# Block spectra of a convolution: tiles of u before tiles of r, and where decoded weights lie meanwhile

## The chip, the core and the metric

The kernel runs on one core of a Trainium2 chip. The metric is the device time of one execution in microseconds (us). A core has five engines with a queue each: TensorE (PE) for matmuls, VectorE (DVE), ScalarE (ACT), GpSimd (POOL) and SyncE (SP), which only sends transfers. Transfers of SP, ACT and POOL run on 16 DMA engines that all share.

## The reference

```python
h_mlp = np.maximum(pos_emb @ w1, 0.0) @ w2
h_filt = h_mlp * np.exp(-0.01 * pos)[:, None]
u = x * v
Uf = np.fft.rfft(u, n=2 * S, axis=1)
Hf = np.fft.rfft(h_filt, n=2 * S, axis=0)
y = np.fft.irfft(Uf * Hf[None, :, :], n=2 * S, axis=1)[:, :S, :]
...
x = (x * y)
h = x @ w_in
g = np.where(h > 0.0, h, np.exp(np.minimum(h, 0.0)) - 1.0)
x = g @ w_out
...
h = x @ w2_in
g = np.maximum(h, 0.0) + alpha * np.minimum(h, 0.0)
out = g @ w2_out
```

There are S = 12480 rows of 128 columns; the inner width of both MLPs is 2048. The weights of the MLPs come as 64-bit floats.

## The kernel before, in words

The Fourier transforms are done as matmuls in two steps. Rows are cut into 98 blocks of 64 positions for each of two halves; the block spectra come first. Three stages follow each other, and the change lies in the first.

**Stage A, positions.** `load_pos` loads the transposed position embeddings into the big region `ureg`. `r_group(g)`, eight times, multiplies them by w1 on PE (eight matmuls) and evicts the result through a Relu to `rreg`, half on ACT, half on DVE. The result is called r: 64 channels of the filter's hidden layer.

**Stage A, block spectra.** `a_tile` takes four channels, does four matmuls with a cosine and sine matrix, and evicts real and imaginary parts. There are 32 tiles of u (128 channels of x times v), written to `ureg`, and 16 tiles of r, written to the regions `sa` and `sb`; every tile of r writes into all of `sa` and `sb`, in strides. The buffers in PSUM are four (`psa`). The list `order` (line 243) alternates: two tiles of u, one of r.

**The ring of x and v.** `load_u(k)` loads x and v of tile k, 98 rows of 2 KB each, on SP's queue; there are five places for x and three for v. `mul_u(k)` multiplies them in the place of x, on POOL, and for every sixth tile on DVE. After tile k of u has been issued, x of tile k+5 is requested (it waits until PE has read tile k), the product of tile k+3 is issued, and v of tile k+6 is requested (it waits until a product has freed a place). SP sends in order, so a transfer that waits holds up all behind it.

**Decoding.** The weights are 16 pieces of 512 KB. `dec_load(j)` loads piece j on SP's queue; `dec_op(j, i)`, eleven steps, turns it into a high and a low part in float32r with six operations on DVE, two on ACT and two on POOL, and writes the two parts to DRAM as another 512 KB (`wd`, pieces 0 to 2 from POOL's queue, 3 to 8 from ACT's). Pieces 0 to 2 are decoded during the position groups, 3 to 8 during the block spectra, 9 at the start of the next stage. `hooks` holds at which tile which step is issued, and `fixed` holds where a piece lies: `ureg`, `dreg`, and columns of `rreg` that are free once their tiles of r have been done.

**Stage B** (`b_r`, `b_u`, `b_h`, `products`, `z_mm`, 25 rounds) finishes the spectra, multiplies them and starts the way back. It starts with `b_r(0)`, which reads the first frequencies of `sa` for all channels, and loads four pieces of the matrix g ahead (`load_g`). **Stage C** is the rest: the last inverse step and both MLPs, tile after tile.

Of the kernel before, what the change touches and what calls it, by code (L numbers as in the profile page):

```python
# [9 lines left out]
F32 = mybir.dt.float32  # L10
# [9 lines left out]
P = 64  # L20
NI = 98
# [4 lines left out]
NF = 99  # L26
# [13 lines left out]
def kernel(ctx: ExitStack, tc: tile.TileContext, posT, w1b, w2b, sc2, xva, xT,  # L40
# [4 lines left out]
    def pool(name, bufs=1, **kw):  # L45
        return tc.tile_pool(name=name, bufs=bufs, reuse_waits="tile", **kw)
# [16 lines left out]
    def col(o, n):  # L63
        return ureg[:, o : o + n]
# [11 lines left out]
    f_sb = fpool.tile([NI, 2 * NF], F32, name="f_sb")  # L76
    dreg = fpool.tile([128, 2048], F32, name="dreg")
    sc_sb = fpool.tile([128, 1], F32, name="sc_sb")
    ups = pb.enter_context(pool("ups", 4, side="right"))
    psa = pb.enter_context(pool("psa", 4, space=PSUM))  # L80


# [51 lines left out]
    def halves(t):  # L134
        return t[:, :1024], t[:, 1024:2048]
# [19 lines left out]
    def load_u(k, t=(0, 1)):  # L155
        for c in t:
            if k < NU:
                u_raw[k, c] = ups.tile([NI, 4, 2, P], F32, name="xv"[c], bufs=(5, 3)[c])
                nc.sync.dma_start(u_raw[k, c].rearrange("i c a p -> i (c a p)"),
                                  xva[:, c, 4 * k : 4 * k + 4].rearrange("i c a p -> i (c a p)"))  # L160

# [7 lines left out]
    def load_pos(g, n=1):  # L169
        nc.sync.dma_start(col(g * GW, n * GW), posT[:, g * GW : (g + n) * GW])  # L170
# [11 lines left out]
            else:  # L182
                nc.scalar.activation(dst, src, AF.Relu)

    w1_sb = col(NG * GW + 4096, 128)
    nc.scalar.dma_start(w1_sb, w1b)
    load_pos(0)
    nc.scalar.dma_start(sc_sb, sc2)
    load_pos(1)
    for j in range(3):  # L190
        fixed[j] = halves(col(NG * GW + 2048 * j, 2048) if j < 2 else dreg)
    dec_load(0)
    load_pos(2, 2)
    dec_load(1)
    load_pos(4, 2)
    nc.sync.dma_start(f_sb, fmat)
    load_u(0)
    load_pos(6, 2)
    load_u(1)
    load_pos(8, 2)  # L200
    dec_load(2)
    load_pos(10, 2)
    load_u(2)
    load_pos(12, 2)
    load_pos(14, 2)
    load_u(3)
    load_u(4)
    nc.sync.dma_start(fw_sb[:NI, : 2 * NF], fwin)
    nc.sync.dma_start(w2_sb, w2b)
    load_u(5, (1,))  # L210
    hooks = {3: [(mul_u, (0,))], 4: [(mul_u, (1,))], 6: [(mul_u, (2, nc.vector))]}
    for j, s in enumerate((0, 1, 4)):
        for i, d in enumerate((0, 0, 0, 0, 0, 0, 0, 1, 1, 1, 2)):
            hooks.setdefault(s + d, []).append((dec_op, (j, i)))
    for g in range(NG // 2):
# [24 lines left out]
                else:  # L240
                    nc.scalar.activation(o, x, AF.Copy, scale=scale)

    order = []
    for k in range(CC // 4):
        order += [(0, 2 * k), (0, 2 * k + 1), (1, k)]
    order = order[:-3] + [order[-1]] + order[-3:-1]

    rfree = [halves(rreg[:, 2048 * x : 2048 * x + 2048]) for x in range(2)]
    fixed.update({9: rfree[1], 3: halves(dreg), 4: rfree[0], 5: halves(dreg), 6: rfree[1], 7: rfree[0], 8: halves(dreg)})
    hooks = dec_plan({3: 1, 4: 12, 5: 17, 6: 24, 7: 28, 8: 33}, (3, 4, 5, 5, 6, 7, 7, 9, 10, 12, 14))  # L250
    hooks.setdefault(40, []).append((dec_load, (9,)))
    gts = {}

    def load_g(d):
# [5 lines left out]
    for t, (kind, k) in enumerate(order):  # L260
        if kind:
            a_tile(r_sb, 4 * k, fw_sb[:NI, : 2 * NF], a_rs, 4 * k, t % 3 != 0, scale=sc_sb, cuts=(0, NR, NF))
            if k == 11 or k == 13:
                load_g(k // 13)
        else:
            a_tile(u_done.pop(k), 0, f_sb, [a_u], 4 * k, t % 3 != 0, cuts=(0, 8, NF) if t == len(order) - 1 else (0, NF))
            load_u(k + 5, (0,))
            if 0 < k < NU - 3:
                mul_u(k + 3, nc.vector if k % 6 == 2 else nc.gpsimd)
            load_u(k + 6, (1,))  # L270
        run_hooks(hooks, t)
    run_hooks(hooks, 99)
# [574 lines left out]
```

## Time and profile before

| | us |
|---|---|
| median of 3 runs | 1430.42 (1430.36 to 1430.6) |
| the profiled execution | 1427.0 |
| its span, first to last instruction | 1425.2 |
| busy in the span: PE | 1384.3 (97%) |
| DVE | 1268.7 (89%) |
| ACT | 1079.9 (76%) |
| POOL | 946.4 (66%) |
| first tile of u on PE starts | 31.83 |
| last tile of the block spectra ends | 108.50 |

A busy share is an average over three stages with different limits. The profile cuts the span into 40 slices of some 36 us: in the first three PE is busy to 0.6, 0.9 and 0.8 and the DMA engines to 0.8, 0.7 and 0.8; from the eleventh slice on the DMA engines are mostly idle and PE is full. The stage that the change touches is the first 108.5 us of 1425.2.

### The profile page before, as it was taken

What the parts mean: (1) busy time and instruction counts of PE and PEld (TensorE: products, weight loads), DVE (VectorE), ACT (ScalarE), POOL (GpSimd) and SP (SyncE); (2) the same over time, 40 slices, a digit from 0 to 9 for tenths busy, and PEclk for the clock granted to TensorE, in tenths of its full rate; (3) what the DMA queues carried; (4) which work ended last, traced back from release to release, by engine and by line L of the source; (5) the groups of instructions that cost most, each with busy time, mean ns of one, the idle gap of its engine ahead of it and who ended that gap; (6) DMA issues with size and microseconds to landing.
All of it is one profiled execution on the core that took longest, in us unless ns stands there. A gap on an engine that the chain in (4) does not pass through costs nothing.

```text
span 1425.2 us, 27157 instructions
## 1 busy us (share of the span) xinstructions
PE 1384.3 (97%) x10156; PEld 1172.9 (82%) x10156; DVE 1268.7 (89%) x1793; ACT 1079.9 (76%) x2041; POOL 946.4 (66%) x840
## 2 busy tenths in 40 slices
PE   6988999999999999999999999999999999999998
PEld 6976777688888888888888888888888888888897
DVE  5677999699999999999999999899999999999997
ACT  2545666488888888888888788887888878888884
POOL 4575788666766667666666666666666666666666
PEclk9999999999999999999999999999999999999999
DMA  8785786560020000000005000000000000000000
GB/s 258 229 261 173 210 236 183 159 191 18 8 83 25 27 18 8 26 26 26 19 8 207 26 26 14 12 25 26 25 15 12 26 25 26 15 11 22 8 8 13
DMA packets 57192, 97.61 MB, mean 68 GB/s; under 512 B 4462, under 2 KB 37298, under 8 KB 55628
## 3 DMA queue, kind: packets, MB, share of 16 engines
q1 hardware_dynamic: 53700, 84.79, 19.6%
q0 software_dynamic: 1440, 7.86, 1.8%
q10 hardware_dynamic: 1920, 3.21, 0.6%
q8 instruction: 80, 1.31, 0.4%
q14 instruction: 52, 0.43, 0.1%
HBM read 70.20 MB, written 25.66 MB: 67 GB/s over the span
## 4 chain that ended last, share of the span: by engine, by line
PE 91%; DMA 4%; ACT 2%; POOL 1%; DVE 1%; issue 1%; SPq 0%; POOLq 0%; ACTq 0%; DVEq 0%
PE psh L575 13%; PE pso L576 13%; PE pso L577 13%; PE psh L576 13%; PE pso L575 13%; PE psh L577 12%; PE psi L475 3%; PE pu L325 3%; PE pzz L388 3%; PE prh L307 2%; DMA x<-in_xva_dram 2%; PE pa L225 2%; PE prh L335 2%; DMA ureg<-in_posT_dram 1%; ACT spreg L338 1%; POOL x L164 1%
## 5 line engine op out<-in xcount | busy, mean ns | idle before, releaser
L598 POOL TENSOR_TENSOR g1l<-ureg,g1h 128x486 fp32r<-128x486 f32 (+3 forms) x313 | 365.1, 1167 | 203.0 <-ACT g1h L624 198.5
L598 POOL TENSOR_TENSOR g2l<-ureg,g2h 128x490 fp32r<-128x490 f32 (+3 forms) x315 | 346.2, 1099 | 118.7 <-ACT g2h L647 45.5
L636 DVE TENSOR_SCALAR ureg<-psh,al_sb 128x486 f32<-128x486 f32 (+3 forms) x416 | 295.9, 711 | 54.4 <-PE psh L577 53.8
L610 ACT ACTIVATE ureg<-psh 128x490 f32<-128x490 f32 (+2 forms) x393 | 225.6, 574 | 91.1 <-PE psh L577 85.5
L641 DVE SCALAR_TENSOR_TENSOR ureg<-psh,ureg 128x486 f32<-128x486 f32 (+3 forms) x416 | 274.1, 659 | 14.3
L618 DVE SCALAR_TENSOR_TENSOR ureg<-ureg,psh 128x486 f32<-128x486 f32 (+3 forms) x416 | 268.3, 645 | 4.5 <-ACT ureg L611 2.9
L624 ACT CAST g1h<-ureg 128x490 fp32r<-128x490 f32 (+3 forms) x405 | 240.0, 593 | 19.9 <-DVE ureg L618 18.4
L611 ACT ACTIVATE ureg<-ureg 128x490 f32<-128x490 f32 (+2 forms) x393 | 239.8, 610 | 12.5
L647 ACT CAST g2h<-ureg 128x490 fp32r<-128x490 f32 (+3 forms) x404 | 234.8, 581 | 8.2 <-DVE ureg L641 6.7
L575 PE MATMUL psh<-sb,sa 128*128 128x486 f32 (+3 forms) x416 | 160.8, 386 | 0.1
L575 PE MATMUL psh<-x2h,sb 128*128 128x486 f32 (+3 forms) x416 | 158.6, 381 | 1.1 <-ACT x2h L667 1.1
L576 PE MATMUL psh<-x2l,sb 128*128 128x486 f32 (+3 forms) x416 | 158.7, 382 | 0.4 <-DVE x2l L668 0.4
L576 PE MATMUL psh<-sb,sa 128*128 128x486 f32 (+3 forms) x416 | 158.8, 382 | 0.0
L577 PE MATMUL psh<-x2h,wc 128*128 128x486 f32 (+3 forms) x416 | 158.3, 381 | 0.0
L577 PE MATMUL psh<-sb,sa 128*128 128x486 f32 (+3 forms) x416 | 157.3, 378 | 0.0
L576 PE MATMUL pso<-g2l,wc 128*128 128x490 f32 (+3 forms) x404 | 155.5, 385 | 0.5 <-POOL g2l L598 0.5
L576 PE MATMUL pso<-g1l,sa 128*128 128x490 f32 (+3 forms) x405 | 155.5, 384 | 0.4 <-DVE g1l L598 0.2
L577 PE MATMUL pso<-g2h,wc 128*128 128x490 f32 (+3 forms) x404 | 154.9, 383 | 0.0
L575 PE MATMUL pso<-g1h,sa 128*128 128x490 f32 (+3 forms) x405 | 154.6, 382 | 0.0
L577 PE MATMUL pso<-g1h,sb 128*128 128x490 f32 (+3 forms) x405 | 154.4, 381 | 0.0
L575 PE MATMUL pso<-g2h,wc 128*128 128x490 f32 (+3 forms) x404 | 154.2, 382 | 0.0
L598 DVE TENSOR_TENSOR g1l<-ureg,g1h 128x490 fp32r<-128x490 f32 (+3 forms) x104 | 122.0, 1173 | 15.1 <-ACT g1h L624 3.6
(134 smaller groups left out, 2386.0 us busy)
## 6 DMA issues: line engine op xcount, KB each, us to landing
rreg<-in_gmat_dram SPq DMA_DIRECT2D x24, 384.0 KB
ureg<-in_finv_dram SPq DMA_DIRECT2D x24, 379.0 KB
ureg<-zhi SPq DMA_DIRECT2D x4, 1584.0 KB
x<-in_xva_dram SPq DMA_DIRECT2D x32, 196.0 KB
v<-in_xva_dram SPq DMA_DIRECT2D x32, 196.0 KB
zlo<-rreg SPq DMA_DIRECT2D x24, 256.0 KB
zhi<-rreg SPq DMA_DIRECT2D x24, 256.0 KB
ureg<-zlo SPq DMA_DIRECT2D x4, 990.0 KB
```

Source lines behind the costliest of these rows:

```text
L325: nc.tensor.matmul(dst, gts[d][rows(half), f - 4 * d, g0 : g0 + 64], src, start=(x == 0), stop=(x == 2))
L575: nc.tensor.matmul(ps[:, :w], ah, bh[:, :w], start=start, stop=False)
L576: nc.tensor.matmul(ps[:, :w], ah, bl[:, :w], start=False, stop=False)
L577: nc.tensor.matmul(ps[:, :w], al, bh[:, :w], start=False, stop=stop)
L598: eng.tensor_tensor(lo[:, :w], e[:, :w], hi[:, :w], ALU.subtract)
L610: nc.scalar.activation(e[:, :w], ps[:, :w], AF.Relu, scale=-1.0)
L611: nc.scalar.activation(e[:, :w], e[:, :w], AF.Exp, scale=-1.0)
L618: nc.vector.scalar_tensor_tensor(e[:, :w], e[:, :w], -1.0, ps[:, :w], op0=ALU.add, op1=ALU.max)
L624: nc.scalar.copy(hi[:, :w], e[:, :w])
L636: nc.vector.tensor_scalar(e[:, :w], ps[:, :w], 0.0, al_sb[:, c : c + 1], op0=ALU.min, op1=ALU.mult)
L641: nc.vector.scalar_tensor_tensor(e[:, :w], ps[:, :w], 0.0, e[:, :w], op0=ALU.max, op1=ALU.add)
L647: nc.scalar.copy(hi[:, :w], e[:, :w])
```

## The change

All tiles of u come first, then all tiles of r, beginning with channels 16 to 63, so that the columns of `rreg` that piece 9 and the first two pieces of g take come free first. `ups`, the pool of places for x and v, becomes one tile `ring` of 4096 columns, with x of tile k in place k mod 5 and v in place 5 + k mod 3, so which place a transfer takes is written down. Pieces 0 to 5 are decoded in the columns of `sa` and `sb`, which nothing else uses until the first tile of r; piece 6 in `dreg`; pieces 7 and 8 in the halves of the ring when u is through; piece 9 in `rreg`. The position loads are moved ahead of the pieces in SP's queue. Every fourth product instead of every sixth goes to DVE.

```diff
--- before.py
+++ after.py
@@ -76,7 +76,7 @@
     f_sb = fpool.tile([NI, 2 * NF], F32, name="f_sb")
     dreg = fpool.tile([128, 2048], F32, name="dreg")
     sc_sb = fpool.tile([128, 1], F32, name="sc_sb")
-    ups = pb.enter_context(pool("ups", 4, side="right"))
+    ring = fpool.tile([128, 4096], F32, name="ring")
     psa = pb.enter_context(pool("psa", 4, space=PSUM))
 
 
@@ -155,7 +155,8 @@
     def load_u(k, t=(0, 1)):
         for c in t:
             if k < NU:
-                u_raw[k, c] = ups.tile([NI, 4, 2, P], F32, name="xv"[c], bufs=(5, 3)[c])
+                o = 512 * (k % 5, 5 + k % 3)[c]
+                u_raw[k, c] = ring[:NI, o : o + 512].rearrange("i (c a p) -> i c a p", c=4, a=2)
                 nc.sync.dma_start(u_raw[k, c].rearrange("i c a p -> i (c a p)"),
                                   xva[:, c, 4 * k : 4 * k + 4].rearrange("i c a p -> i (c a p)"))
 
@@ -182,34 +183,36 @@
             else:
                 nc.scalar.activation(dst, src, AF.Relu)
 
-    w1_sb = col(NG * GW + 4096, 128)
+    w1_sb = col(NG * GW, 128)
     nc.scalar.dma_start(w1_sb, w1b)
     load_pos(0)
     nc.scalar.dma_start(sc_sb, sc2)
     load_pos(1)
-    for j in range(3):
-        fixed[j] = halves(col(NG * GW + 2048 * j, 2048) if j < 2 else dreg)
+    slots = [halves(t[:, 2048 * x : 2048 * x + 2048]) for t in sregs for x in range(3)]
+    fixed.update({j: slots[j] for j in range(6)})
+    load_pos(2, 2)
+    load_pos(4, 2)
     dec_load(0)
-    load_pos(2, 2)
-    dec_load(1)
-    load_pos(4, 2)
+    load_pos(6, 2)
     nc.sync.dma_start(f_sb, fmat)
     load_u(0)
-    load_pos(6, 2)
+    load_pos(8, 2)
+    dec_load(1)
+    load_pos(10, 2)
     load_u(1)
-    load_pos(8, 2)
+    load_pos(12, 2)
     dec_load(2)
-    load_pos(10, 2)
+    load_pos(14, 2)
     load_u(2)
-    load_pos(12, 2)
-    load_pos(14, 2)
-    load_u(3)
-    load_u(4)
+    load_u(3, (0,))
+    load_u(4, (0,))
+    dec_load(3)
     nc.sync.dma_start(fw_sb[:NI, : 2 * NF], fwin)
     nc.sync.dma_start(w2_sb, w2b)
-    load_u(5, (1,))
-    hooks = {3: [(mul_u, (0,))], 4: [(mul_u, (1,))], 6: [(mul_u, (2, nc.vector))]}
-    for j, s in enumerate((0, 1, 4)):
+    hooks = {}
+    for k, s in enumerate((3, 5, 6)):
+        hooks[s] = [(mul_u, (k,)), (load_u, (k + 3, (1,)))]
+    for j, s in enumerate((2, 4, 6)):
         for i, d in enumerate((0, 0, 0, 0, 0, 0, 0, 1, 1, 1, 2)):
             hooks.setdefault(s + d, []).append((dec_op, (j, i)))
     for g in range(NG // 2):
@@ -240,15 +243,16 @@
                 else:
                     nc.scalar.activation(o, x, AF.Copy, scale=scale)
 
-    order = []
-    for k in range(CC // 4):
-        order += [(0, 2 * k), (0, 2 * k + 1), (1, k)]
-    order = order[:-3] + [order[-1]] + order[-3:-1]
-
-    rfree = [halves(rreg[:, 2048 * x : 2048 * x + 2048]) for x in range(2)]
-    fixed.update({9: rfree[1], 3: halves(dreg), 4: rfree[0], 5: halves(dreg), 6: rfree[1], 7: rfree[0], 8: halves(dreg)})
-    hooks = dec_plan({3: 1, 4: 12, 5: 17, 6: 24, 7: 28, 8: 33}, (3, 4, 5, 5, 6, 7, 7, 9, 10, 12, 14))
-    hooks.setdefault(40, []).append((dec_load, (9,)))
+    order = [(0, k) for k in range(NU)] + [(1, k) for k in (4, 5, 6, 7, 8, 9, 10, 11, 12, 13, 14, 15, 0, 1, 2, 3)]
+
+    fixed.update({6: halves(dreg), 7: halves(ring[:, 2048:]), 8: halves(ring[:, :2048]), 9: halves(rreg[:, 2048:4096])})
+    hooks = {}
+    for j, s, t in ((3, None, 2), (4, 1, 9), (5, 9, 16), (6, 16, 24), (7, 30, 33), (8, 32, 37), (9, 38, None)):
+        if s is not None:
+            hooks.setdefault(s, []).append((dec_load, (j,)))
+        for i, d in enumerate((0, 1, 2, 2, 3, 4, 4, 6, 7, 8, 10)):
+            if t is not None:
+                hooks.setdefault(t + d, []).append((dec_op, (j, i)))
     gts = {}
 
     def load_g(d):
@@ -260,13 +264,13 @@
     for t, (kind, k) in enumerate(order):
         if kind:
             a_tile(r_sb, 4 * k, fw_sb[:NI, : 2 * NF], a_rs, 4 * k, t % 3 != 0, scale=sc_sb, cuts=(0, NR, NF))
-            if k == 11 or k == 13:
-                load_g(k // 13)
+            if k == 10 or k == 12:
+                load_g(k // 12)
         else:
-            a_tile(u_done.pop(k), 0, f_sb, [a_u], 4 * k, t % 3 != 0, cuts=(0, 8, NF) if t == len(order) - 1 else (0, NF))
+            a_tile(u_done.pop(k), 0, f_sb, [a_u], 4 * k, t % 3 != 0, cuts=(0, NF))
             load_u(k + 5, (0,))
             if 0 < k < NU - 3:
-                mul_u(k + 3, nc.vector if k % 6 == 2 else nc.gpsimd)
+                mul_u(k + 3, nc.vector if k % 4 == 2 else nc.gpsimd)
             load_u(k + 6, (1,))
         run_hooks(hooks, t)
     run_hooks(hooks, 99)
```

PE's queue at the start (pa is a buffer of PSUM; f_sb stands for a tile of u, fw_sb for a tile of r; x128 is 32 tiles of four matmuls). Before:

```order
L175 MATMUL pa<-ureg 98x128 x64
L225 MATMUL pa<-f_sb,x 128x198 x8
L225 MATMUL pa<-fw_sb,rreg 128x198 x4
L225 MATMUL pa<-f_sb,x 128x198 x8
L225 MATMUL pa<-fw_sb,rreg 128x198 x4
```

Now:

```order
L176 MATMUL pa<-ureg 98x128 x64
L228 MATMUL pa<-f_sb,ring 128x198 x128
L228 MATMUL pa<-fw_sb,rreg 128x198 x64
L311 MATMUL prh<-rreg,sa 64x128 x16
L339 MATMUL prh<-w_sb,rreg 64x128 x16
```

The sixteen tiles of r, four matmuls each, have moved from between the tiles of u to behind the last, right ahead of the next stage's first matmuls (prh).

SP's queue from its start (in_posT are positions, in_wo and in_wi pieces of weights, in_xva x and v). Before:

```order
L170 DMA ureg<-in_posT_dram 128x392 x2
L91 DMA ureg<-in_wo_dram 128x1024
L170 DMA ureg<-in_posT_dram 128x784
L91 DMA ureg<-in_wo_dram 128x1024
L170 DMA ureg<-in_posT_dram 128x784
L196 DMA f_sb<-in_fmat_dram 98x198
```

Now:

```order
L171 DMA ureg<-in_posT_dram 128x392 x2
L171 DMA ureg<-in_posT_dram 128x784 x2
L91 DMA sa<-in_wo_dram 128x1024
L171 DMA ureg<-in_posT_dram 128x784
L197 DMA f_sb<-in_fmat_dram 98x198
```

And now from piece 3 to the last of x and v:

```order
L91 DMA sb<-in_wo_dram 128x1024
L210 DMA fw_sb<-in_fwin_dram 98x198
L211 DMA w_sb<-in_w2b_dram 128x128
L160 DMA ring<-in_xva_dram 98x512 x7
L91 DMA sb<-in_wi_dram 128x1024
L160 DMA ring<-in_xva_dram 98x512 x16
L91 DMA sb<-in_wi_dram 128x1024
L160 DMA ring<-in_xva_dram 98x512 x14
L91 DMA dreg<-in_wi_dram 128x1024
L160 DMA ring<-in_xva_dram 98x512 x19
```

Two more loads of positions stand ahead of the first piece, and behind the start only three pieces (4, 5 and 6) stand between transfers of x and v, where six did before.

POOL's queue over the tiles of u now (L165 is a product, L124 and L126 are the two steps of decoding):

```order
L165 TENSOR_TENSOR ring<-ring 98x512 x7
L124 TENSOR_TENSOR sb<-sb 128x512
L126 TENSOR_TENSOR sb<-sb 128x512
L165 TENSOR_TENSOR ring<-ring 98x512 x5
L124 TENSOR_TENSOR sb<-sb 128x512
L165 TENSOR_TENSOR ring<-ring 98x512
L126 TENSOR_TENSOR sb<-sb 128x512
L165 TENSOR_TENSOR ring<-ring 98x512 x4
L124 TENSOR_TENSOR sb<-sb 128x512
L165 TENSOR_TENSOR ring<-ring 98x512
L126 TENSOR_TENSOR sb<-sb 128x512
L165 TENSOR_TENSOR ring<-ring 98x512 x3
```

Six steps of decoding (pieces 3, 4 and 5) stand between the products; those of pieces 6, 7 and 8 have moved behind the last product.

## Rows read from the trace of the kernel before

**Rows 1.** Windows: start:end, length, busy us (instructions) per engine, PE clock, DMA share, GB/s.

```profile
0.00:20.00 20.00, 13.08 (x76) 12.00 (x77) 9.25 (x16) 5.81 (x9) 4.90 (x8) 1.00 0.91 264
20.00:40.00 20.00, 15.92 (x103) 15.55 (x102) 12.41 (x18) 6.93 (x14) 10.52 (x10) 0.91 0.79 252
40.00:60.00 20.00, 20.00 (x121) 19.79 (x119) 11.47 (x22) 11.34 (x27) 11.92 (x10) 1.00 0.72 224
60.00:80.00 20.00, 16.69 (x90) 14.48 (x88) 15.58 (x24) 8.59 (x21) 13.35 (x10) 1.00 0.75 217
80.00:100.00 20.00, 16.01 (x89) 14.57 (x89) 16.89 (x29) 11.70 (x29) 14.17 (x11) 1.00 0.93 290
...
42.00:52.00 10.00, 10.00 (x62) 10.00 (x61) 8.46 (x14) 6.31 (x15) 7.36 (x6) 1.00 0.72 225
54.00:62.00 8.00, 7.76 (x45) 7.09 (x43) 3.42 (x7) 3.94 (x10) 3.84 (x3) 1.00 0.94 296
```

**Rows 2.** Timeline of PE: start, us, engine, line, operation, tiles [idle before <-releaser].

```profile
26.66 5.34 PE L175 MATMUL pa<-ureg 128*98 128x128 f32 x32 [2.39 <-DMA ureg<-in_posT_dram]
31.83 2.85 PE L225 MATMUL pa<-f_sb,x 98*128 98x198 f32 x16
34.51 1.50 PE L225 MATMUL pa<-fw_sb,rreg 98*128 98x198 f32 x8
35.85 2.84 PE L225 MATMUL pa<-f_sb,x 98*128 98x198 f32 x16
...
105.66 2.84 PE L225 MATMUL pa<-f_sb,x 98*128 98x198 f32 x16
108.43 1.10 PE L307 MATMUL prh<-rreg,sa 64*64 64x128 f32 x32
```

**Rows 3.** Waits from 32 to 108 us: who <- for whom: us, times, longest.

```profile
POOL x L164 <- DMA x<-in_xva_dram: 24.5, 13, 6.1
...
DVE rreg L105 <- DMA rreg<-in_wi_dram: 7.2, 2, 4.0
```

**Rows 4.** Timeline, a turn of the ring: products on POOL, requests on SP.

```profile
41.89 1.28 POOL L164 TENSOR_TENSOR x<-x,v 98x512 f32<-98x512 f32 x1 [1.55 <-DVE dreg L105]
43.19 0.32 SPq L159 DMA_DIRECT2D v<-in_xva_dram  x1
43.56 0.38 SPq L159 DMA_DIRECT2D x<-in_xva_dram  x1
47.80 1.44 POOL L164 TENSOR_TENSOR x<-x,v 98x512 f32<-98x512 f32 x1 [0.71 <-DMA x<-in_xva_dram]
49.19 1.27 POOL L124 TENSOR_TENSOR dreg<-dreg 128x512 f32<-128x512 f32 x1
53.89 1.27 POOL L164 TENSOR_TENSOR x<-x,v 98x512 f32<-98x512 f32 x1 [0.32 <-DMA x<-in_xva_dram]
```

**Rows 5.** Transfers issued from 42 to 52 us.

```profile
v<-in_xva_dram SPq DMA_DIRECT2D x4, 196.0 KB
x<-in_xva_dram SPq DMA_DIRECT2D x4, 196.0 KB
```

**Rows 6.** Timeline: the product of tile 4 on POOL; a product on DVE.

```profile
31.63 1.35 POOL L164 TENSOR_TENSOR x<-x,v 98x512 f32<-98x512 f32 x1
66.72 0.69 DVE L164 TENSOR_TENSOR x<-x,v 98x512 f32<-98x512 f32 x1 [0.36 <-DMA x<-in_xva_dram]
```

**Rows 7.** Transfers issued from 0 to 108 us, with their sizes.

```profile
x<-in_xva_dram SPq DMA_DIRECT2D x32, 196.0 KB
...
rreg<-in_wi_dram SPq DMA_DIRECT2D x3, 512.0 KB
wd_wi<-rreg ACTq DMA_DIRECT2D x3, 512.0 KB
```

**Rows 8.** Timeline: a piece requested, one written back, and the product behind them.

```profile
52.76 0.35 SPq L91 DMA_DIRECT2D rreg<-in_wi_dram  x1
53.60 0.58 ACTq L128 DMA_DIRECT2D wd_wo<-dreg  x1
58.31 1.27 POOL L164 TENSOR_TENSOR x<-x,v 98x512 f32<-98x512 f32 x1 [3.15 <-DMA x<-in_xva_dram]
```

**Rows 9.** Timeline: eviction of r, ACT's first copies of the next stage, PE's third round.

```profile
105.86 0.43 ACT L241 ACTIVATE sa<-pa,sc_sb 128x200 f32<-128x200 f32 x1 [0.68 <-PE pa L225]
109.61 1.54 ACT L311 COPY rreg<-prh 64x256 f32<-64x256 f32 x4 [0.51 <-PE prh L307]
118.53 1.10 PE L307 MATMUL prh<-rreg,sa 64*64 64x128 f32 x32 [1.13 <-ACT spreg L338]
```

**Rows 10.** Windows view, a stretch of the next stage.

```profile
180.00:200.00 20.00, 18.86 (x500) 14.71 (x496) 19.79 (x25) 13.37 (x26) 16.55 (x14) 1.00 0.77 223
```

## The prediction, made before the change was run

> **What bounds the kernel now.** First the windows view, in steps of 20 us [rows 1]. The reader is to see two things. From 40 us to 100 us TensorE (PE) is busy 20.0, 16.7 and 16.0 of 20 us, so it waits a little, at a granted clock of 1.00. The DMA engines meanwhile are at a share of 0.72 to 0.93, moving 224, 217 and 290 GB/s. Neither is idle, neither is full: in this stage transfers and matmuls share the time. Then the timeline of PE [rows 2]: the position groups end at 26.66 + 5.34 = 32.0 us, tiles of u start at 31.83, two of u and one of r take 35.85 - 31.83 = 4.02 us (**1.34 us a tile**, of either kind), and the last tile ends at 105.66 + 2.84 = **108.5 us**. 48 tiles of 1.34 us are 64.3 us; the stage took 76.7. The waits view says who was late [rows 3]: POOL, which multiplies x by v, waited 24.5 us for x to land, thirteen times; VectorE waited 7.2 us, twice, for a piece of weights.
>
> So what limits a tile of u is a ring, and the timeline shows one turn of it [rows 4]. POOL's product at 41.89 ends at 43.17; at 43.19 SP may send for the v that takes the freed place, at 43.56 for its x; the product of these two starts at 47.80, after waiting for x. The next turn ends at 53.89. There are three places for v, so a turn serves three tiles: 5.91 and 6.09 us, **2.0 us a tile**. Nothing but x and v moved meanwhile (four of each between 42 and 52 us [rows 5]), at 225 GB/s [rows 1].
>
> **The change, part by part.** The sum goes by the path that will set the end of the stage: product of tile 4, product of tile 31, then PE alone.
>
> Positions ahead of the weights: PE could start tile 0 some us sooner. I cost this at nothing. Tiles 0 to 4 are loaded early in both versions, but tile 31 waits for product 31, and products go at the pace of the ring. If the ring were no limit, it would be worth the 2.39 us that PE waited for positions before 26.66 [rows 2] and lesser waits ahead of it.
>
> Product of tile 4: before at 31.63, done at 32.98 [rows 6]. Its v now stands behind one more piece of weights (four, not three). A piece is 512 KB [rows 7], at the 290 GB/s of the best 20 us [rows 1] 1.8 us; as positions and u otherwise come in the same amount, I take half of it and say **34 us** (33 to 35).
>
> 27 more tiles of u: the ring keeps its sizes, five places for x and three for v, and v of tile k+6 still waits for the product of tile k+3. The fixed places take out one thing: v never waits for a younger product. VectorE takes a quarter of the products instead of a sixth, at 0.69 us instead of 1.27 [rows 6]. What goes away between these tiles is r: PE no longer needs 2.01 us for each tile of u, but 1.34. The pace is the unknown. From above: 2.0 us, the turn in the trace [rows 4]. From below: the stretch from 54 to 62 us, share 0.94, 296 GB/s [rows 1], in which four loads had piled up behind a piece of weights; 0.40 MB a tile (twice 196 KB [rows 7]) would go through in 1.36 us. Below that lies nothing, as PE needs 1.34. I take **1.85 us**, nearer the turn, because the piling up that made 296 GB/s cannot last with three places for v. 27 x 1.85 = 50.0 us.
>
> Pieces 4, 5 and 6 are loaded in SP's queue between these tiles, and pieces 3, 4 and 5 written back from ScalarE's. Around 53 us one piece was loaded and one written between two products, which then lay 58.31 - 53.89 = 4.42 us apart instead of 2.0 [rows 4, 8]: 2.4 us for such a pair, three pairs **7.2 us**. In bytes alone a load would be 1.8 us, 5.4 for three.
>
> After product 31 PE has one tile of u and sixteen of r, with nothing left to load for them: 17 x 1.34 = 22.8, and 0.3 us allowed for its start and its drain: **23.1 us**. Before, all sixteen ran between tiles of u, while the next of these were still on their way.
>
> The sum: 34 + 50.0 + 7.2 + 23.1 = 114.3 us, against 108.5: +5.8.
>
> The hand-over to the next stage: before, r's last tile ran ahead of the last two of u, and the first matmuls of the next stage started at 108.43, beside the last evictions [rows 2]; ScalarE's copies of them began at 109.61, 1.1 us after PE's last tile [rows 9]. Now they read what the very last tile writes: an eviction of 0.43 us [rows 9], then 1.10 us of matmuls [rows 2], then the copies, some 1.8 us after PE's last tile: **+0.7 us**. The matrix w now waits for the last tile in SP's queue, with two loads of g behind it; the first to read those two starts at 118.53 [rows 9], 10 us after the hand-over, so nothing.
>
> Decoding: pieces 3 to 6 are loaded about eight tiles ahead of their first use, so VectorE's 7.2 us of waiting should vanish. Worth nothing here: it had delayed evictions and so PE, and PE is no longer what is late. Pieces 7 and 8 go into the ring in r's time; VectorE and ScalarE have room there. The next stage has VectorE at 19.79 of 20 us [rows 10], no slack for catching up, so the delay is passed on whole.
>
> In all +6.5 us. The profiled execution took 1427.0 us (span 1425.2), so 1433.5 for one like it; the median of the runs is 3.4 us above it, and the forecast for the median is 1430.4 + 6.5 = **1436.9 us**.
>
> **The rivals.** A measurement of this kernel tells changes from about 0.2%, here 2.9 us.
>
> *The queue stays full (faster).* Without r's matmuls between them, products follow each other sooner, and SP always has loads waiting, so the 296 GB/s of 54 to 62 us becomes the rule. It decides from a pace of 1.5 us a tile. From product 4 on 14.2 MB are to be moved (27 tiles, 3 pieces in, 3 to 4 out [rows 7]): 48 us at 296 GB/s, so 34 + 48 + 23.1 + 0.7 = 105.8, that is -2.7 us, 1427.7, and a bit less with a quicker start. For it: four loads waiting did give that rate. Against: no 20 us of the stage held it. The Trainium skill, page "DMA: Bandwidth & Descriptors", section "Where 436 GB/s comes from", puts the limit of a core's transfers from HBM at about 358 GB/s; no stretch of 20 us here shows that. By that figure the whole load would hide behind PE, and as an estimate the stage would end about 15 us sooner, near 1415. Chance 0.10.
>
> *About even.* A pace midway between 1.36 and 2.0, 1.68 us: 34 + 45.4 + 7.2 + 23.1 + 0.7 = 110.4, +1.9 us, 1432.3. For it: fixed places for v and more products on VectorE both shorten the turn. Against: in the turn of [rows 4] v did not wait for a younger product, and it still took 2.0. The same page of the Trainium skill, section "Why a DMA increments its semaphore by 16 and not by 1", says that a transfer is split over the largest number of engines up to 16 that divides its rows, which makes 14 for the 98 rows of x and v. Their share could then be 0.875 at most, and [rows 1] shows 0.72 from 42 to 52 us, so the trace is below that cap and something else held it. As an estimate by the cap alone the pace would be 2.0 x 0.72 / 0.875 = 1.65 us, which is this rival. Chance 0.22.
>
> *Slower still.* POOL's six halves of decoding now stand between products that follow closely, without r's time to absorb them: each 1.27 us [rows 6] that is passed on in full adds up to 7.6 us to the forecast's middle, about 1444. Against: one such stood at 49.19 [rows 4], and the turn around it was no longer than the one before. Chance 0.12.
>
> *The change does not do what it says.* If the pieces in the ring come late in r's time, VectorE stands before evictions and r's tiles stretch; four buffers of PSUM cover about three tiles of that, 4.0 us. It is part of the upper end.
>
> **How the numbers follow.** Forecast (pace 1.7 to 2.0, +3 to +10 us) 0.56, faster 0.10, about even 0.22, slower still 0.12. So faster by over 0.2% has 0.10, within 0.2% 0.22, slower 0.56 + 0.12 = 0.68. The range from 1428.0 to 1442.5 leaves out most of the first rival and the third. The even case and the forecast alone span 1428 to 1441.
>
> **What would show it.** Right: POOL's or VectorE's products 1.7 to 2.0 us apart from 34 to about 91 us, POOL waiting for x before most; the DMA share high until 91 us and low during r's tiles; those 1.34 us each with PE full; the next stage's first matmuls near 115 us; its length unchanged. Wrong: products 1.4 us apart and PE full from 28 us on; or r's tiles with waits for VectorE or ScalarE; or a changed time after the hand-over.

## The result, and the profile after

The changed kernel took **1441.7 us** (median of 4, 1440.3 to 1444.4), the kernel before on the same chip 1430.5: a ratio of **1.0078, 95% interval 1.0056 to 1.0101, +11.2 us**. It is slower, as forecast; the forecast was 1436.9, and 1441.7 lies inside its range of 1428.0 to 1442.5, near the upper end. The profiled execution took 1444.4 us (span 1442.6), the slowest of the four, while the profiled one of before was 3.5 us under its median; so the two traces lie 17.4 us apart, 6 us more than the medians.

Windows of the changed kernel (columns as in [rows 1]), with three of its stretches apart:

```profile
20.00:40.00 20.00, 14.65 (x78) 12.99 (x77) 13.65 (x20) 6.61 (x14) 13.00 (x12) 0.83 0.83 262
40.00:60.00 20.00, 16.91 (x82) 14.79 (x80) 13.38 (x21) 7.66 (x16) 10.80 (x8) 0.91 0.79 246
60.00:80.00 20.00, 15.68 (x60) 15.05 (x61) 8.81 (x13) 5.69 (x12) 11.64 (x9) 0.68 0.76 233
80.00:100.00 20.00, 17.66 (x82) 16.47 (x82) 9.59 (x15) 7.68 (x16) 12.89 (x10) 0.84 0.63 193
100.00:120.00 20.00, 20.00 (x117) 20.00 (x116) 12.60 (x30) 14.95 (x42) 4.41 (x4) 0.96 0.40 142
...
61.50:71.00 9.50, 9.41 (x29) 9.08 (x30) 2.92 (x4) 2.80 (x6) 5.35 (x6) 0.51 0.67 200
102.00:121.00 19.00, 19.00 (x115) 19.00 (x115) 12.60 (x30) 15.34 (x43) 5.41 (x4) 1.00 0.35 126
126.00:132.40 6.40, 5.22 (x92) 4.39 (x88) 1.18 (x3) 2.48 (x5) 2.55 (x2) 0.52 0.30 113
```

Read the last three columns. While tiles of u run (to 98 us) the DMA share is 0.63 to 0.83. That is 0.01 to 0.07 more than in the same windows of [rows 1] up to 80 us, and 0.30 less from 80 to 100. While tiles of r run (102 to 121) PE is full and the DMA engines are at 0.35. That is the shape that was forecast. The clock column was not: it stood at 1.00 from 40 to 100 us in [rows 1], and here it falls to half (1.2 GHz) again and again.

PE's timeline (columns as in [rows 2]):

```profile
26.42 2.85 PE L228 MATMUL pa<-f_sb,ring 98*128 98x198 f32 x16
31.99 4.93 PE L228 MATMUL pa<-f_sb,ring 98*128 98x198 f32 x16 [2.73 <-issue]
...
61.59 14.23 PE L228 MATMUL pa<-f_sb,ring 98*128 98x198 f32 x56 [2.82 <-POOL ring L165]
78.54 11.17 PE L228 MATMUL pa<-f_sb,ring 98*128 98x198 f32 x48 [2.73 <-POOL ring L165]
...
98.51 23.07 PE L228 MATMUL pa<-fw_sb,rreg 98*128 98x198 f32 x128
122.09 0.45 PE L311 MATMUL prh<-rreg,sa 64*64 64x128 f32 x8 [0.52 <-ACT sa L244]
```

Eight records are one tile. Tiles of u begin at 26.42, 5.4 us sooner than before, and the sixteen of r only at 98.51; they end at 121.58. The longest stretches at half clock follow PE's waits of 2.7 to 2.8 us: the seven tiles from 61.59 take 14.23 us, 2.03 each instead of 1.34.

How the first tiles were held, on VectorE and POOL, and two later products:

```profile
26.03 0.50 DVE L105 TENSOR_SCALAR sa<-sa 128x512 uint32<-128x512 uint32 x1
31.20 0.68 DVE L182 TENSOR_SCALAR rreg<-pa 98x512 f32<-98x512 f32 x1
32.03 1.27 POOL L124 TENSOR_TENSOR sa<-sa 128x512 f32<-128x512 f32 x1 [2.29 <-ACT sa L122]
36.04 2.51 POOL L165 TENSOR_TENSOR ring<-ring 98x512 f32<-98x512 f32 x2
43.17 1.27 POOL L165 TENSOR_TENSOR ring<-ring 98x512 f32<-98x512 f32 x1 [4.62 <-PE pa L228]
...
95.49 1.30 POOL L165 TENSOR_TENSOR ring<-ring 98x512 f32<-98x512 f32 x1 [1.91 <-DMA ring<-in_xva_dram]
```

With positions ahead, piece 2 comes later: its first step on VectorE is at 26.03. Its steps stand ahead of an eviction of positions (31.20), which frees the buffer for tile 2 of u (31.99, shown as "issue"), and its two on POOL stand ahead of the products of tiles 4 and 6 (36.04). So the product of tile 4 ends at 37.3 us, against 33.0 [rows 6]. The product of tile 31 ends at 95.49 + 1.30 = 96.8.

The waits from 32 to 108 us, the lines that answer to [rows 3]:

```profile
POOL ring L165 <- DMA ring<-in_xva_dram: 18.7, 11, 3.6
DVE ring L165 <- DMA ring<-in_xva_dram: 8.9, 5, 4.7
POOL ring L165 <- PE pa L228: 6.6, 3, 4.6
```

VectorE's 7.2 us of waiting for pieces of weights are gone; in their place it waits 8.9 us for x and v, as it has more products. The last line looks like a wait for PE to give back a place of x. It is not: its longest wait, 4.6 us, is that of the product of tile 7 at 43.17, and SP's queue shows that x of this tile was requested only at 38.25, right behind piece 4:

```profile
37.72 0.48 SPq L91 DMA_DIRECT2D sb<-in_wi_dram  x1
38.25 1.27 SPq L160 DMA_DIRECT2D ring<-in_xva_dram  x3
```

PE had read the tile in that place (tile 2) before 36.92, the end of its row above. So the transfer was what came late; the view names PE because one of its matmuls ended at the same moment. The two shorter waits of that line are of the same kind. With these POOL waited 25.3 us for x and v, about as long as before (24.5 [rows 3]). SP in turn waited for POOL. From 32 to 98 us, in SP's own queue:

```profile
SPq L160 <- POOL ring L165: 26.7, 16, 3.6
```

Sixteen times the next load stood until a product had freed a place, 26.7 us in all: that is the ring of the prediction.

ACT's copies of the next stage, the first ones, which answer to [rows 9], and the fourth group, after and (last line) before:

```profile
123.82 1.54 ACT L315 COPY rreg<-prh 64x256 f32<-64x256 f32 x4 [1.47 <-PE prh L311]
141.46 1.54 ACT L315 COPY rreg<-prh 64x256 f32<-64x256 f32 x4 [1.28 <-PE prh L311]
124.81 1.53 ACT L311 COPY rreg<-prh 64x256 f32<-64x256 f32 x4 [1.28 <-PE prh L307]
```

The first begin 2.24 us after PE's last tile, where it was 1.11.

| us, profiled executions | before | forecast | after |
|---|---|---|---|
| product of tile 4 done | 33.0 | 34.0 | 37.3 |
| product of tile 31 done | | 91.2 | 96.8 |
| PE's last tile ends | 108.5 | 114.3 | 121.6 |
| ACT's first copies of the next stage | 109.6 | 116.1 | 123.8 |
| its fourth group of these copies | 124.8 | | 141.5 |
| end of the span | 1425.2 | | 1442.6 |

Of the 17.4 us, 13.1 are in the block spectra, 1.1 in the hand-over, 2.4 in the next stage's first rounds, at half clock until 132.4, and the rest later in that stage.

### The profile page after: what moved, and what is told of

It is laid out like the page before. It is cut to its first block, busy times and chain, and to the rows that moved or that the text cites. A ratio compares the mean times of both kernels' runs of the same rounds, so it can differ in the third digit from the quotient of the medians.

```text
span 1442.6 us, 27133 instructions
## 1 busy us (share of the span) xinstructions
PE 1398.1 (97%) x10156; PEld 1185.6 (82%) x10156; DVE 1264.2 (88%) x1789; ACT 1082.3 (75%) x2044; POOL 943.2 (65%) x839
## 4 chain that ended last, share of the span: by engine, by line
PE 89%; DMA 4%; POOL 2%; DVE 2%; ACT 1%; issue 1%; SPq 0%; POOLq 0%; ACTq 0%; DVEq 0%
PE psh L579 13%; PE pso L580 13%; PE pso L581 12%; PE psh L580 12%; PE pso L579 12%; PE psh L581 12%; PE psi L479 3%; PE pu L329 3%; DMA ring<-in_xva_dram 2%; PE pzz L392 2%; PE pa L228 2%; PE prh L311 2%; PE prh L339 2%; ACT spreg L342 1%; DMA sa<-in_wo_dram 1%
```

## The experiments

Theories: *order* (tiles of u wait for transfers, and r's matmuls no longer cover any), *ring* (few places hold transfers back), *transfers* (they go no faster however many wait), *clock*, *start* and *hand-over*. Twelve kernels were run. Where one has extra matmuls, their results are not read.

### 1. Clock: matmuls that keep PE busy

```diff
+    def fill(n, ps=None):
...
+            nc.tensor.matmul(ps[:, : 2 * NF], f_sb[:, :128], f_sb, start=True, stop=True)
...
+        fill(n, ps)
...
+                   n={2: 7, 15: 7, 22: 7, 31: 4}.get(k, k > 2))
...
+    fill(8)
```

> The changed kernel, with extra matmuls on PE that nothing reads: one ahead of each tile of u from tile 3 on, four to seven ahead of tiles 2, 15, 22 and 31 (where the changed kernel's PE timeline has its waits of 1.6 to 2.8 us), eight behind the last tile of r. Theory clock: in the changed kernel the granted clock fell to half after each of these waits, so that tiles of u took 2.8 instead of 1.4 us, POOL waited 6.6 us for PE to give places of x back, the first 3.4 us of r's tiles and 6.8 us at the start of the next stage ran at half clock; with PE kept busy the clock stays at 1.00 and the time falls by 5 to 9 us, to 1433 to 1437 (the forecast's own terms). Theory order: tiles of u wait for transfers anyhow and the half clock lies in time that PE would have idled; the time stays at 1440 to 1443.

Measured: 1442.9 us, ratio 1.008 (1.0065 to 1.0095), no gain. Two windows and two rows of PE's timeline:

```profile
40.00:97.00 57.00, 52.19 (x300) 49.46 (x299) 29.27 (x47) 20.95 (x44) 32.68 (x26) 1.00 0.75 233
97.00:119.00 22.00, 22.00 (x133) 22.00 (x133) 13.28 (x32) 16.44 (x45) 7.40 (x6) 1.00 0.38 132
```

```profile
97.81 21.60 PE L234 MATMUL pa<-fw_sb,rreg 98*128 98x198 f32 x128
122.03 1.10 PE L319 MATMUL prh<-rreg,sa 64*64 64x128 f32 x32
```

The clock stands at 1.00, and still r's tiles begin at 97.81 instead of 98.51. So, by these two traces, half clock cost the tiles of u no more than 0.7 us: it lay in time that PE would have waited. (The 6.6 us that the expectation calls a wait for PE were waits for transfers, as shown above.) It cost r's tiles 1.5 us (21.60 instead of 23.07) and the next stage's first rounds 2.4 (its fourth group of copies here is 13.6 us behind before's, as its first one is). The eight matmuls behind the last tile gave 2 us of that back, since the next stage's first ones had to wait for them. The clock theory falls, except for some 4 us of a profiled execution behind the tiles of u.

### 2. Transfers: three pieces less to load

The first form let all three pieces share one place, so that each waited for the last one's write-back:

```diff
+        if 4 <= j <= 6:
+            parts[j] = parts[3]
+            return
```

> The changed kernel without the loads of pieces 4, 5 and 6; their decoding runs over the data of piece 3, so three pieces of weights come out wrong. Theory order (tiles of u go at the pace of the transfers): 1.5 MB less in front of x and v is worth 5 us (three times 1.8 us by bytes), and the two waits of 2.7 to 2.8 us on PE at 59 and 76 us go, with the half clock behind them: 1433 to 1437. Rival, the ring's turn (places, products, PE) sets the pace and a load of weights passes beside it: within 2 us of the changed kernel, 1440 to 1443.

1452.4 us, ratio 1.0146 (1.0131 to 1.0161): PE waited 7.2 us for VectorE behind those decoding steps. It tells nothing of transfers, and shows what a decoding chain costs in the way of products. In the second form `parts[3]` became `parts[j - 4]`:

> The changed kernel without the loads of pieces 4, 5 and 6; their decoding runs over the places of pieces 0 to 2, which were written back long before, so three pieces come out wrong and no step of decoding waits for another piece (which made the first kernel of this kind useless). Theory transfers (tiles of u go at the pace of what SP's queue brings): 1.5 MB less ahead of x and v is worth 5 us and the two long waits of PE at 59 and 76 us with it: 1434 to 1437. Rival, the ring's turn sets the pace and a load of weights passes beside it: 1440 to 1443.

1443.0 us, ratio 1.0086 (1.0059 to 1.0112). The total is no lower; the trace says why, in PE's timeline and a row of the waits from 85 to 122 us:

```profile
92.97 9.54 PE L231 MATMUL pa<-fw_sb,rreg 98*128 98x198 f32 x56
105.88 14.92 PE L231 MATMUL pa<-fw_sb,rreg 98*128 98x198 f32 x72 [3.37 <-DVE sb L243]
```

```profile
ACT sa L247 <- DMA wd_wi<-sa: 3.1, 1, 3.1
```

r's tiles begin at 92.97, **5.5 us sooner**, close to the 5.4 that three times 1.8 us by bytes gives. Then they wait 3.4 us, because piece 6 now lay in `sa`, where r's first tiles are to be written, and PE fell to half clock after the wait. The experiment's own flaw ate the gain. So, by this one trace, a piece of weights in SP's queue delays the tiles of u by the time of its bytes; it does not pass beside them.

### 3. Ring: six more places each for x and v

```diff
-                o = 512 * (k % 5, 5 + k % 3)[c]
+                at[k, c] = free[c].pop(0)
...
+            m = max(0, min(6, k - 2))
...
+                free[0].append(sregs[0][:, o : o + 512])
+                free[1].append(sregs[0][:, o + 512 : o + 1024])
```

> The changed kernel with six more places for x and six more for v, in the first half of r's region, which is free between the write-back of pieces 0 to 2 and the first tile of r; transfers are issued eleven tiles ahead instead of five. Theory ring (three places for v hold transfers back): the DMA share between 40 and 90 us rises from 0.63 to 0.79 to over 0.9, products come 1.5 us apart, the time falls by 7 us or more, to 1435 or less. Theory transfers (loads of 98 rows do not go faster however many wait): the pace stays near 1.85 us and the time within 3 us of the changed kernel.

1438.5 us, ratio 1.005 (1.0035 to 1.0065): 3 to 4 us less than the changed kernel, with intervals that just overlap, and between what the two theories expected. Windows, PE, and SP's wait for POOL from 32 to 98 us:

```profile
40.00:60.00 20.00, 17.19 (x85) 16.82 (x84) 13.39 (x17) 7.62 (x17) 12.73 (x10) 0.83 0.93 277
60.00:80.00 20.00, 15.22 (x63) 14.36 (x62) 12.45 (x18) 6.12 (x14) 10.30 (x9) 0.77 0.75 220
```

```profile
92.86 21.60 PE L232 MATMUL pa<-fw_sb,rreg 98*128 98x198 f32 x128
```

```profile
SPq L160 <- POOL ring L169: 3.2, 2, 2.6
```

With more places SP waits 3.2 us for POOL instead of 26.7, and the share rises to 0.93. So the three places for v did hold transfers back. From 60 us on the share falls back, at half clock, while VectorE waits 6.8 us for a piece that now stands behind more x and v. r's tiles begin 5.7 us sooner. Ring and clock are looked at together in 6.

### 4. Order: the old order with the rest of the change

In the kernel before, `ring` with its fixed places, the positions ahead, and every fourth product on VectorE; the order of tiles and the places of all pieces as before:

```diff
-    ups = pb.enter_context(pool("ups", 4, side="right"))
+    ring = fpool.tile([128, 4096], F32, name="ring")
...
-                mul_u(k + 3, nc.vector if k % 6 == 2 else nc.gpsimd)
+                mul_u(k + 3, nc.vector if k % 4 == 2 else nc.gpsimd)
```

> The kernel before with the change's ring of fixed places, its order of position loads and first pieces, and every fourth product on VectorE; the order of tiles and the places of pieces 3 to 9 stay as before. Theory order (putting r's tiles last costs all of it): 1428 to 1431.5, as before or up to 2.4 us less. Rival, part of the cost lies in fixed places or in positions ahead (pieces and v come later): 1433 or more.

1432.9 us, ratio 1.0009 (0.9995 to 1.0023): between the two cases, and by the interval the same as before. So these parts bring nothing and cost at most some 3 us; the order with its places for decoding costs the rest.

### 5. r put back, and the hand-over

Eleven tiles of r among the last eleven of u:

```diff
-    order = [(0, k) for k in range(NU)] + [(1, k) for k in (4, 5, 6, 7, 8, 9, 10, 11, 12, 13, 14, 15, 0, 1, 2, 3)]
+    order = [(0, k) for k in range(21)]
+    for k in range(11):
+        order += [(0, 21 + k), (1, k)]
+    order += [(1, k) for k in range(11, 16)]
```

> The changed kernel with eleven tiles of r put back between tiles 21 to 31 of u (one behind each), five left for the end; to free r's regions by then, piece 5 is decoded earlier, piece 6 in dreg, pieces 7 and 8 in columns of rreg and in dreg. Theory order (r's matmuls cost their full 1.34 us because no transfer runs beside them): tile 20 ends near 76 us as now, then 27 tiles of 1.34 us, 36 us, so the stage ends near 112 instead of 121.6 and the time falls by 8 to 11 us, to 1430.5 to 1434. Rival, the cost lies in the pace of u's tiles itself, which r's between them slow down as much as they use: a fall of 4 us or less, 1437 or more.

1442.7 us, ratio 1.0092 (1.0074 to 1.011). A miss by the time, half a hit by the trace. (Piece 5 is written back behind the first tile of r here and holds values of r.)

```profile
76.21 1.50 PE L228 MATMUL pa<-fw_sb,rreg 98*128 98x198 f32 x8
...
107.84 8.20 PE L228 MATMUL pa<-fw_sb,rreg 98*128 98x198 f32 x48
```

Tile 21 of u ends at 76.2, a little sooner than expected, and from 88 us on u and r alternate without waits. But an eviction into `sb` waited 3.3 us for piece 5's write-back, and PE 2.5. The last tile ends at 116.0, 5.5 us sooner, not 10; the next stage then began at half clock, and in the medians nothing is left.

The hand-over: two rounds of u's matmuls ahead of and behind the first `b_r`.

```diff
+    us = {0: b_u(0)}
     b_r(0)
+    us[1] = b_u(1)
```

> The changed kernel with the next stage's first two rounds of u's matmuls (b_u, which read nothing of r) put ahead of and behind b_r of round 0, where PE waited 0.5 us for the last evictions and 1.7 us for copies and then ran at half clock for 6.8 us. Theory hand-over: what the stage's start costs (0.7 us forecast, about 3 to 4 us in the changed kernel's trace, half clock included) comes back, 1437.5 to 1439.5. Rival, VectorE sets the pace of the next stage and PE's start is covered: 1441 to 1443.

1442.9 us, ratio 1.0089 (1.0067 to 1.0111): nothing. PE is at 1.00 from 120 to 134 us now, and at half from 134.3 to 140.5:

```profile
134.30:140.50 6.20, 3.64 (x64) 3.25 (x68) 2.93 (x4) 2.31 (x5) 4.38 (x4) 0.54 0.26 107
```

The slow rounds were put off, not avoided. Whether the hand-over costs anything apart from the clock was not told apart.

### 6. Ring and clock together, the start, and a version built from them

The deeper ring of 3 with `fill`, ten, six, six and four ahead of tiles 2, 7, 17 and 21, one ahead of the others, two at the end:

> The deeper ring of the run before (six more places each for x and v, 1438.5) together with extra matmuls that nothing reads, one ahead of each tile of u, four to ten ahead of tiles 2, 7, 17 and 21, and two behind the last tile of r. Theory clock: with more transfers under way PE is nearer to being the limit, so the half clock that this kernel had at 41 to 48, 54 to 61, 64 to 67 and 74 to 81 us and at the start of the next stage costs time here: 1433 to 1436. Rival, PE still waits for decoding steps and transfers: 1437 to 1440.

1435.4 us, ratio 1.0033 (1.0018 to 1.0049), **2 to 3 us less than the ring alone**, though the two intervals overlap. Fill was worth nothing in 1 and seems worth something here. PE was full from 32 to 114 us, some 17 us of it fill (52 matmuls of 0.335 us), while the last of x and v was requested by 81 us; so PE may have been held by the fill itself, which the last run of this section tries. A window:

```profile
60.00:80.00 20.00, 20.00 (x121) 20.00 (x120) 17.89 (x20) 7.67 (x16) 15.93 (x12) 1.00 0.91 295
```

The start, by itself: piece 2 decoded among the first tiles of u.

```diff
-    for j, s in enumerate((2, 4, 6)):
+    for j, s in enumerate((2, 4)):
...
+    for j, s, t in ((2, None, 1), (3, None, 5), (4, 1, 10), (5, 9, 16), (6, 16, 24), (7, 30, 33), (8, 32, 37), (9, 38, None)):
```

> The changed kernel with the decoding of piece 2 moved from behind the seventh position group to the first tiles of u (pieces 3 and 4 one to three tiles later). In the changed kernel its seven steps on VectorE start at 26.0 us, 5 us later than before, and stand ahead of the last evictions of positions (31.2 and 32.5 us), so PE waits 2.7 us for a buffer, and its two steps on POOL stand ahead of the product of tile 4 (36.0 us instead of the 34 less 1.35 of the forecast). Theory start: the product of tile 4 comes 2 to 3 us sooner and the time falls by 2 to 4 us, to 1438 to 1439.5. Rival, transfers set the pace from the first tile on, so a sooner start is lost again by tile 31: 1440.5 to 1443.

1440.2 us, ratio 1.0056 (1.0035 to 1.0077), which overlaps the changed kernel's. The product of tile 4 (33.35 + 1.27) now ends at 34.6 us, 2.7 sooner, and r's tiles begin at 99.46, no sooner:

```profile
33.35 1.27 POOL L165 TENSOR_TENSOR ring<-ring 98x512 f32<-98x512 f32 x1 [3.88 <-DMA ring<-in_xva_dram]
...
99.46 22.71 PE L228 MATMUL pa<-fw_sb,rreg 98*128 98x198 f32 x128
```

In this execution, the slowest of its six and 4 us above their median, the gain at the start was lost again by tile 31, as the rival says; the median is 1.5 us under the changed kernel's, which the intervals do not tell from nothing.

Deep ring, late piece 2 and less fill in one; pieces 2, 5 and 6 also get other places, and 5 and 6 are loaded and decoded earlier, so more than the fill differs from the run of 1435.4:

```diff
+                   n={2: 4, 7: 4}.get(k, 2 < k < 17))
...
+    fill(4)
```

> The parts that helped, together: six more places each for x and v, extra matmuls that nothing reads only ahead of tiles 2 to 16 of u (four ahead of tiles 2 and 7, one ahead of the others) and four behind the last tile of r, piece 2 decoded behind the position groups. In the run with a deeper ring and more extra matmuls PE was full from 32 to 114 us, 16.8 us of it extra ones, while the last x and v had been loaded by 84 us. Theory: with some 8 us of them gone PE reaches the last tile of u at 85 to 87 us, the last of r at 107 to 109, and the time is 1428 to 1432, level with the kernel before. Rival, tiles of u then wait for transfers and decoding after all, at half clock: 1433 to 1438.

1443.3 us, ratio 1.008 (1.0057 to 1.0102): a clear miss. Two places show it. The first, on VectorE and POOL:

```profile
53.02 8.08 DVE L169 TENSOR_TENSOR sa<-sa 98x512 f32<-98x512 f32 x1
54.33 1.33 POOL L169 TENSOR_TENSOR sa<-sa 98x512 f32<-98x512 f32 x1
55.55 1.33 POOL L124 TENSOR_TENSOR sb<-sb 128x512 f32<-128x512 f32 x1
56.77 1.32 POOL L169 TENSOR_TENSOR ring<-ring,sa 98x512 f32<-98x512 f32 x1
57.99 1.34 POOL L126 TENSOR_TENSOR sb<-sb 128x512 fp32r<-128x512 f32 x1
59.22 1.32 POOL L169 TENSOR_TENSOR ring<-ring 98x512 f32<-98x512 f32 x1
```

A product that takes VectorE 0.69 us [rows 6] took 8.08, and ended only when POOL paused. PE waited 8.0 us for it. The second, on VectorE:

```profile
86.55 0.43 DVE L105 TENSOR_SCALAR sb<-sb 128x512 uint32<-128x512 uint32 x1 [6.43 <-DMA sb<-in_wi_dram]
```

PE's other long wait, 6.7 us until 89.31 for a product on VectorE, was no hold: that product took 0.70 us, but stood in VectorE's queue behind this decoding step, which waited 6.4 us for its piece. The obvious remedy for the first, in this kernel:

```diff
-                mul_u(k + 3, nc.vector if k % 4 == 2 else nc.gpsimd)
+                mul_u(k + 3, nc.gpsimd)
```

> The run before it (deeper ring, few extra matmuls, piece 2 late; 1443.3) with every product from tile 4 on on POOL and none on VectorE. In that run a product on VectorE, 0.69 us by itself, took 8.08 us at 53.0 while POOL worked without a pause from 54.3 to 60.5, and PE waited 8.0 us for it; a second wait of 6.7 us for a product on VectorE followed at 82.6. Theory: VectorE's instruction is held while POOL's follow each other; without products on VectorE both waits go, and the time falls by 9 us or more, to 1430 to 1434. Rival, POOL with all products and the halves of decoding becomes the limit, or VectorE's decoding and evictions are held in the same way: 1438 or more.

1442.2 us, ratio 1.0086 (1.007 to 1.0102): the rival. The hold fell on a decoding step instead:

```profile
55.91 10.43 DVE L114 TENSOR_SCALAR sb<-sb 128x512 uint32<-128x512 uint32 x1
```

0.43 us of work took 10.43, while POOL ran eight instructions from 56.17 to 66.05 without a pause. VectorE's evictions stood behind it, so PE's buffers did not come free.

Last, the kernel of 1435.4 with less fill, and decoding left where it was:

```diff
-                   n={2: 10, 7: 6, 17: 6, 21: 4}.get(k, k > 2))
+                   n={2: 8, 7: 6, 17: 2}.get(k, 2 < k < 17))
```

> The deeper ring with extra matmuls (1435.4) with fewer of these: eight ahead of tile 2, six ahead of tile 7, two ahead of tile 17, one ahead of the other tiles from 3 to 16, none later, and four behind the last tile of r instead of two; decoding as in that run. Theory: there PE was full from 32 to 114 us, so 6.7 us less of extra matmuls end the last tile of u at 86 to 88 us instead of 92, and the time falls by 3 to 6 us, to 1429.5 to 1432.5, level with the kernel before. Rival, behind tile 17 products and transfers are no earlier than PE needed them there, waits and half clock take the place of the extra matmuls: 1434 to 1437.

1434.4 us, ratio **1.0016 (1.0000 to 1.0033)**, lowest run 1428.5. By windows and PE:

```profile
40.00:60.00 20.00, 19.53 (x116) 18.99 (x115) 12.92 (x19) 7.78 (x17) 13.31 (x10) 1.00 0.93 267
45.00:56.00 11.00, 11.00 (x66) 10.77 (x66) 6.54 (x10) 4.91 (x10) 7.63 (x7) 1.00 0.93 254
60.00:80.00 20.00, 17.72 (x98) 15.84 (x97) 13.46 (x18) 8.24 (x18) 13.42 (x12) 1.00 0.94 283
```

```profile
89.92 21.60 PE L238 MATMUL pa<-fw_sb,rreg 98*128 98x198 f32 x128
```

The DMA share is over 0.9 for 40 us, the clock 1.00, and r's tiles begin at 89.9, 8.6 us sooner than in the changed kernel, not at 86 to 88. The time falls by 7 to 9 us against the changed kernel, and by 4 to 5 against the ring alone, here with intervals apart; against the run of 1435.4 nothing can be told. From 45 to 56 us nothing but x and v moved, the share stood at 0.93, and they came at 254 GB/s: 0.40 MB a tile are then 1.6 us. (With the ring alone it was 266 GB/s from 43 to 52 us, 1.5 us a tile.) So the theory *transfers* holds in part: with places enough, x and v by themselves came at 1.5 to 1.6 us a tile, not at 1.36. No version beat the kernel before: this one is at best level with it.

## Why the prediction was right in sign and too small

**The mechanism held.** Products between 37 and 97 us waited for x and v, and SP for products to free places; the DMA share was high until then and low after; r's tiles ran without a gap; and the old order with the change's other parts lost nothing that can be measured (4). That r's time alone, without transfers, costs what the old order had hidden is only half shown: with eleven tiles of r put back the last tile ended 5.5 us sooner, but the medians did not fall (5).

**Product of tile 4, "34 us"**: 37.3. The step priced positions ahead at nothing and the piece ahead of v at half its transfer. It missed that decoding of piece 2 moves with its load and stands ahead of evictions and of this product. Yet the term itself was less of a base than the sum made it: with piece 2 decoded later the product came 2.7 us sooner, and in that one trace nothing was left of it by tile 31 (6). The sum started its count at that product; by that trace what ran through was the queue of transfers.

**27 tiles at 1.85 us and three pairs of 2.4 us, 57.2 us**: 59.5 from product 4 to product 31, 2.3 more. The loads' share of the pairs was right in size: 5.5 us for three (2). Writes alone were not tried. That pace stayed near the ring's turn of [rows 4] because of the places: with six more of each SP's waits for POOL fell from 26.7 to 3.2 us, the share rose to 0.93 and over, and r's tiles began 5.7 to 8.6 us sooner. So the queue-stays-full rival describes a kernel that the change is not: with the deeper ring and fill (1435.4 us) the 296 GB/s it asked for was nearly held for 20 us, 295 from 60 to 80. But pieces of weights moved in that window, as they did in the stretch at 296 GB/s of [rows 1]. For x and v alone the bound from below, 1.36 us a tile, was too low: at 254 to 266 GB/s, with the share flat at 0.93, it is 1.5 to 1.6 us (6).

**PE alone, "23.1 us"**: from 96.8 to 121.6 are 24.8. 1.34 us a tile held (21.60 for sixteen at full clock, with fill), but here the first ran at half clock: 23.07.

**Hand-over, "+0.7"**: +1.1, 2.24 us from the last tile to the first copies instead of the 1.8 forecast.

**"The delay is passed on whole"**: not quite. The next stage's first rounds ran at half clock in the profiled execution, another 2.4 us. This is the missing term: the prediction read the granted clock of 1.00 in [rows 1] as given, though the change opens waits of nearly 3 us on PE. For the tiles of u that was all but harmless (1); behind them nothing covers it.

Together, terms that were off in the profiled execution: 3.3 at tile 4, 2.3 in pace, 1.7 in PE alone, 0.4 in the hand-over and 2.4 in the next stage, 10.1 us, and about 1 us more later. By the medians the forecast was short by 4.8 us; which of these a median execution has in full can't be told, as only the slowest of the changed kernel's four has a trace. All these terms are off in the same direction; that 1441.7 still lies in the range owes more to the range's width, 14.5 us, than to the sum.

**The rivals.** "About even" needed a pace of 1.68; the three places for v kept the changed kernel from it. Its cap of 0.875 on the share of such transfers does not stand in the traces either: with x and v alone the share was 0.93 for 11 us (6). The estimate of 1415 beside the first rival does not come out of the prediction's own sum, which gives about 1419; it entered neither the range nor a chance. "Slower still" put its 7.6 us on POOL's decode halves: POOL's six halves did stand between products, but POOL still waited 25 us for x and v, so the time came out on that rival's side for other reasons. Pieces in the ring in r's time were no trouble: PE was full from 102 to 121.

## What to carry to other kernels

When transfers feed one kind of tile and another kind needs none, the second is the cover for the first. Put at the end, here, it ran for its full 23 us beside DMA engines at a share of 0.35, and a gain must come from transfers that really run faster without it, which takes places for them to land in. A step whose cost is "nothing, since PE waits anyway" should be priced with what it does to the clock behind the wait, too. A wait that a view puts down to an engine is to be checked against the time at which that engine had done its part. And a chain of small steps that moves with a load is to be followed on each engine's queue, with the evictions and products behind it.

## What the runs showed that was not expected

An instruction of VectorE can be held until POOL pauses: 8.08 us for a product of 0.69, 10.43 us for a decoding step of 0.43. Not every one is: in the first of these two runs, at 49.54 and beside POOL at work, a decoding step of 0.43 us took 1.38. What makes the long ones was not found. In the changed kernel itself one product on VectorE took 2.23 us:

```profile
71.72 2.23 DVE L165 TENSOR_TENSOR ring<-ring 98x512 f32<-98x512 f32 x1 [0.54 <-DMA ring<-in_xva_dram]
```

The Trainium skill, page "SBUF — State Buffer", section "Who interferes with whom", says that VectorE and GpSimd share a pair of ports as an exclusive lock, and that the second to issue blocks until the first has finished. By that rule the hold would end with one POOL instruction, some 1.3 us; the traces agree that VectorE blocks, and the 1.38 us fit that, but the two long ones show it held through five of them and more.

Keeping PE's clock at 1.00 with extra matmuls was worth nothing that the medians show where transfers set the pace (1), and 4 to 5 us where more of them were under way (the last run of 6 against the ring alone), though each such matmul also takes PE's time.
